# Sinkhorn attention into a routed expert layer: the last transposes of attention move to DMA, and loads, logits and sums move with them

## The chip, the core and the metric

One Trainium2 chip, one core. The engines named below are PE (TensorE: matrix products, with its weight loads PEld), DVE (VectorE), ACT (ScalarE), POOL (GpSimd) and SP (SyncE, which here only issues DMAs). The metric is the device time of one execution in microseconds (us); lower is better. Each engine runs its own instructions in the order in which they were built into its queue and waits, at an instruction, for semaphores that other engines or DMAs raise.

## The reference, cut to what matters

Two stages. The first is attention inside blocks of 96 rows, with the blocks of k and v mixed by an 8x8 matrix P per head; the second sends every row of the result x through all 8 experts, weighted by a balanced softmax.

```python
B, H, S, D = 4, 8, 768, 64               # P: 5 rounds of exp, row and column sums
k_sorted = einsum('bhij,bhjcd->bhicd', P, k_blocks)
v_sorted = einsum('bhij,bhjcd->bhicd', P, v_blocks)
attn = softmax(q_block @ k_sorted_block.T / 8)          # per block of 96
x = (attn @ v_sorted_block) as [B*S = 3072, H*D = 512]

logits = x @ w_gate                      # 8 experts
P = exp(logits - max)
for _ in range(8):                       # balance rows, then columns
    P /= P.sum(1); P /= P.sum(0); P *= N / E
for e in range(8):
    out += P[:, e:e+1] * (relu(x @ w1[e]) @ w2[e])      # 512 -> 1024 -> 512
```

## The kernel before

Batches are counted from 0 in the code, so "batches 3 and 4" of the change are the code's `bb` 2 and 3; below they are batch 2 and batch 3. A unit `hp` is a pair of heads (0 to 3).

**Attention of one batch.** `load_batch` (L70) fetches q, k and v of a batch from HBM as bf16; these DMAs are issued by POOL, each into one of five shared buffers `kvq`. `spread_r` (L151) makes R, the matrix P of the batch spread over 128 partitions, by two POOL multiplications (L139); R lies in two buffers used in turn by even and odd batches. `sort_values` (L162) multiplies v by R on PE (L165), ACT copies the result into `vs` (L167), and `hop` (L155) moves it by eight small DMAs into `vsb`, four issued by SP and four by POOL. Then, per head pair: `queries` (L174) has POOL lay out q again as `qr` (L186, two buffers), PE transpose it (L190) and ACT or DVE copy it out; `keys` (L196) multiplies k by R (L204), with the DVE copy L209; `scores` (L218) is L226 with the exp on ACT (L234); `mix` (L237) is L244, with DVE dividing by the row sums into `og` (L247, L248).

**Turning x.** The result `og` has rows on partitions; the expert stage wants it transposed, in `xtT`. `turn` (L252) does it with eight PE transposes into one PSUM bank and a DVE copy (L258); `turn_by_dma` (L260) has SP issue one transposing DMA (L261). `logits` (L268) multiplies `xtT` by the gate, 24 small matmuls (L275), and DVE copies them to `glog` (L279).

**The order of the work** is written by hand. A plan string per batch lists the steps of each group: `q`, `k`, `s`, `m` with a head pair, `t` for `turn`, `T` for `turn_by_dma`, `x` for one of the four DVE subtractions of `sum_x(0)` (L121, L128), `L` for all logits of the batch before, `l` for logits of this one. `weave` (L546) alternates the groups with steps of `ex`, which is the first expert's work on the batches already done (`hidden0` L402, `output0` L411). So PE goes back and forth between a batch's attention and expert 0 of the batch before. What is wrapped in `pin` keeps the order in which it was written on its engine; the rest (the copies to `qr`, the DMAs of `hop` for batches 2 and 3, the transposing DMAs) is placed by the scheduler. PSUM is eight banks in rotation (`pa`) during this stage, then split anew into five (`bk`) and three (`op`).

**The first expert's tail.** The loop at L873 has 56 steps: `last_two` does expert 0 for batches 2 and 3, `balance` (L653, the eight rounds of the router's P on `glog`, one PE matmul L681 and some DVE operations per round) is advanced at the steps listed at L883, and `hiddens` starts the other experts at step 27. `scale0` (L829) scales expert 0's outputs on ACT once P is final; `sums(8)` (L887) starts the POOL sums of the second weights, held back by a small copy of `glog`. After the loop the seven other experts follow, with seven products in place of eight for each 2x2 block product: some 500 us in which nothing is changed.

Of the kernel before, what the change touches and what calls it, by code (L numbers as in the profile page):

```python
# [25 lines left out]
def kernel(  # L26
# [14 lines left out]
    N, Dm, E, F = 3072, 512, 8, 1024  # L41
    NT = 24
    TB = S // 128
# [26 lines left out]
    def load_batch(bb, parts):  # L70
        for x, l0, n in parts:
            d, src = {"v": (vt, v), "k": (kt, k), "q": (qt, q)}[x]
            if bb not in d:
                d[bb] = kvp.tile([128, 8, 384], BF16, name="kvq", bufs=5)
            pin(nc.gpsimd.dma_start(
                out=d[bb][:, l0:l0 + n, :],
                in_=src[bb, l0:l0 + n].rearrange("h (p kk) d -> p h (kk d)", kk=6)))
# [43 lines left out]
    def sum_x(p):  # L121
        if p not in xc:
            xc[p] = xcp.tile([128, 3, 2, 512], BF16, name="xc", bufs=2)
        ta, tb = (slice(1024 * p + 512 * i, 1024 * p + 512 * i + 512) for i in range(2))
        b11, b12, b21, b22 = (xtT[:, k:k + 2, t] for k in (0, 2) for t in (ta, tb))
        x1, x2, x4 = (xc[p][:, j] for j in range(3))
        for a, b, c in ((b12, b11, x1), (b22, x1, x2), (b21, x2, x4), (b22, b12, b12)):
            pin(nc.vector.tensor_tensor(out=c, in0=a, in1=b, op=ALU.subtract))  # L128
            yield
# [4 lines left out]
    def build_r(bb, eng, n, pbps=None):  # L134

        Rt[bb] = perp.tile([128, 8, 8, 16], BF16, name=f"R{bb % 2}")
        for h in range(0, 8, n):
            yield
            ins = eng.tensor_tensor(  # L139
                out=mkap(Rt[bb], [Rt[bb].ap[0], [16, 8 * n], [1, 16]] if pbps is None else  # L140
                         [Rt[bb].ap[0], [128, n], [16, 8], [1, 16]], off=h * 128),
                in0=(mkap(Pb, [Pb.ap[0], [1, 8 * n], [0, 16]], off=(bb * 8 + h) * 8)
                     if pbps is None else
                     mkap(pbps, [pbps.ap[0], [1, n], [32, 8], [0, 16]], off=h)),
                in1=mkap(mask16, [mask16.ap[0], [0, 8 * n], [1, 16]] if pbps is None else
                         [mask16.ap[0], [0, n], [0, 8], [1, 16]]),
                op=ALU.mult)
            pin(ins)


    def spread_r(bb):  # L151
        for _ in build_r(bb, nc.gpsimd, 4):
            pass
# [59 lines left out]
    x0 = sum_x(0)  # L213
# [54 lines left out]
    def logits(bb, bank, ks):  # L268

        if 0 in ks:  # L270
            gp[bb] = bank([128, TB, E], F32)
        for kk in ks:
            for t in range(TB):
                c = bb * S + t * 128
                pin(nc.tensor.matmul(gp[bb][:, t, :], xtT[:, kk, c:c + 128], wg[:, kk],  # L275
                                     start=(kk == 0 and t == 0), stop=(kk == 3),
                                     skip_group_check=True))
        if 3 in ks:
            nc.vector.tensor_copy(glog[:, bb * TB:(bb + 1) * TB, :], gp[bb])  # L279
# [122 lines left out]
    def hidden0(c0, hTs, hbank, fbs=range(8)):  # L402
        for fb in fbs:
            hps = hbank()
            for kk in range(4):
                pin(nc.tensor.matmul(hps[:, 0:384], w1t[0][:, kk, fb * 128:(fb + 1) * 128],  # L406
                                     xtT[:, kk, c0:c0 + 384], start=(kk == 0), stop=(kk == 3)))
            nc.scalar.activation(out=hTs[:, fb, 0:384], in_=hps[:, 0:384], func=AF.Relu)
            yield

    def output0(c0, hTs, obank, done, tts=range(3)):  # L411
        for tt in tts:
            oacc = obank()
            for fb in range(8):
                pin(nc.tensor.matmul(oacc, hTs[:, fb, tt * 128:(tt + 1) * 128],  # L415
                                     w2t[0][:, fb, :], start=(fb == 0), stop=(fb == 7)))
                if fb == 3:
                    yield
            done(c0 // 128 + tt, oacc)
            yield  # L420
# [21 lines left out]
    with tc.tile_pool(name="ps0", bufs=4, space=bass.MemoryType.PSUM,  # L442
# [71 lines left out]
        for x in ("s00 k2 s01 k3 p s02 s03 m00 s10 m01 s11 m02 t00 m03 s12 m10 t01 s13 h00 m11 "  # L514
                  "g00 m12 h01 g01 m13 t10 h02 g02 t11 h03 g03 v0 v1 v2 v3 h10 g10 l").split():
            n = [int(c) for c in x[1:]]
# [10 lines left out]
            elif x[0] == "g":  # L527
                b, g, t = *n, part[x[1:]]
# [17 lines left out]
    def weave(a, b, na, nb):  # L546

        t = 0
        for i in range(na):
            next(a, 0)  # L550
            while t * na < (i + 1) * nb:
                next(b, 0)
                t += 1

    with ExitStack() as c2:
        pa = c2.enter_context(tc.tile_pool(name="pa", bufs=8, space=bass.MemoryType.PSUM,
                                           reuse_waits="tile"))
        bank1 = lambda shape, dt: pa.tile(shape, dt, name="bank", tag="bank")
        ebank = lambda: bank1([128, 512], F32)
        def by_turns(x, y):  # L560
            for a, b in ((x, y), (x, y)):
                yield next(a)
                yield next(b)

        def first_two():
            yield from hidden0(384, halves[1], ebank, range(2, 8))
            for c0, hTs in ((0, halves[0]), (384, halves[1])):
                o = [output0(c0, hTs, ebank, keep, (tt,)) for tt in range(3)]
                if c0 == 0:
                    yield from by_turns(o[0], o[1])  # L570
                    yield from o[2]
                else:
                    for one in o:
                        yield from one
            for c0 in (S, S + 384):
                hTs = mps.tile([128, 8, 384], BF16, name="hTs")
                yield from hidden0(c0, hTs, ebank)
                yield from output0(c0, hTs, ebank, keep)

        ex = first_two()  # L580

        def run(n):
            for _ in range(n):
                next(ex)

        def run_both(a, counts):
            for n in counts:
                next(a, 0)
                run(n)

        at1 = attention(1, bank1, "k0 k1 q0 q1 s0 k2 q2 k3 q3 s1 s2 s3 "
                                  "m0 m1,t0 m2,t1 m3,t2 t3,l0 l3")
        run_both(at1, (1, 1, 1, 0, 1, 0, 0, 1, 0, 1, 0, 2))
        load_batch(2, [(x, 0, 8) for x in "vkq"])
        spread_r(2)
        run_both(at1, (2, 1, 1, 1))
        run_both(sort_values(2, bank1), (1, 0, 1, 0, 1))
        run_both(at1, (1, 1))
        for bb, plan, ns in (
                (2, "q0,q1,k0 q2,x0,k1,s0 q3,x0,k2,s1 m0,T0 k3,s2 m1,T1,x0 s3 m2,T2 m3,T3",  # L600
                 (6, 4, 2, 2)),
                (3, "q0,q1,k0 q2,k1,s0 q3,k2,s1 m0,T0 k3,s2,L0 m1,T1 s3 m2,T2 m3 t3,l0 l3",
                 (6, 4, 0, 4))):
            at1 = attention(bb, bank1, plan)
            weave(at1, ex, 5, ns[0])
            if bb + 1 < B:
                load_batch(bb + 1, [(x, 0, 8) for x in "vkq"])
                spread_r(bb + 1)
            else:
                load_w1(1)  # L610
                sums = sum_w(1)
            weave(at1, ex, 3, ns[1])
            if bb + 1 < B:
                weave(sort_values(bb + 1, bank1), ex, 5, ns[2])
            else:
                for _ in sums:
                    pass
            weave(at1, ex, 3 if bb == 3 else 1, ns[3])
        for _ in ex:
            pass  # L620
    actx.close()
# [15 lines left out]
    def bank():  # L637
        return bk.tile([128, 512], F32, name="bk")
# [190 lines left out]
    def scale0(ts):  # L829
        for t in ts:  # L830
            pin(nc.scalar.activation(out=acc(t), in_=acc(t), func=AF.Copy,
                                     scale=glog[:, t, 0:1]))
# [36 lines left out]
    tail0, chain, ahead = last_two(), balance(), hiddens()  # L869
    x1, x2 = sum_x(1), sum_x(2)  # L870
    works = {12: x0, 18: x1, 22: x1, 25: x1, 26: x1, 41: x2, 43: x2, 46: x2, 48: x2}
    scaled = {41: 0, 42: 4, 43: 1, 45: 5, 47: 2, 49: 6}
    for n in range(56):  # L873
        next(tail0)
        if n >= 27:
            next(ahead)
            if n == 50:
                sum_h(0, hTs[0], 0, 3)
        if n in works:
            next(works[n], 0)  # L880
        if n in scaled:
            scale0([scaled[n]])
        if n in (0, 2, 4, 7, 8, 12, 14, 17, 19, 22, 24, 26, 28, 30, 32, 34, 36, 38):  # L883
            next(chain)
        if n == 40:
            pin(nc.gpsimd.tensor_copy(held, glog[0:96, NT - 1, 0:2]))
            sums(8)  # L887

# [2 lines left out]
    for n in range(1, 3 * (E - 1) + 1):  # L891
        e, p, hT = 1 + (n - 1) // 3, (n - 1) % 3, hTs[n - 1]
# [55 lines left out]
```

## Time and profile before

| what | value |
|---|---|
| time, median of 3 runs | 667.61 us (667.38 to 668.79) |
| the profiled execution | 667.94 us, span 666.2 us |
| PE busy | 652.2 us, 98% of the span |
| DVE, POOL, ACT busy | 83%, 71%, 45% |
| attention and expert 0 of batches 0 to 3 | about 0 to 163 us |
| the seven other experts | from about 163 us to the end |

The span runs from the first to the last instruction; the execution's own time has some 1.7 us around it. In a row of the timeline the columns are the start in us, the length in us, the engine, the line, the operation, what it writes and reads, its sizes and the number of instructions merged into the row; a bracket tells how long the engine sat idle before it and what ended that.

### The profile page before, as it was taken

How to read it: one execution, taken by the hardware profiler on the slowest of the kernel's cores; microseconds unless marked ns; L12 is line 12 of the kernel's file. 1: busy time of each engine (PE TensorE's matmuls, PEld its weight loads, DVE VectorE, ACT ScalarE, POOL GpSimd, SP SyncE). 2: the span in 40 equal slices, each digit the busy share in tenths (PEclk: the TensorE clock that was granted, in tenths of full speed). 3: DMA queues.
4: the chain of work that ended last, by engine and by line, in shares of the span. 5: the costliest groups of instructions: out<-in, count | busy, mean ns of one | idle time of the engine just before them, and what ended most of it. 6: DMA issues, size and time to landing. Idle time of an engine off the chain costs nothing.

```text
span 666.2 us, 13041 instructions
## 1 busy us (share of the span) xinstructions
PE 652.2 (98%) x5007; PEld 432.8 (65%) x5084; DVE 555.3 (83%) x1120; ACT 300.5 (45%) x535; POOL 470.9 (71%) x500
## 2 busy tenths in 40 slices
PE   7999999999999999999999999999999999999997
PEld 3766665554666666666666666666666666666666
DVE  6655866785888898898989898989898989898996
ACT  5775874476455443333334333433343334333430
POOL 4713254037897898898897999689886999646652
PEclk9999999999999999999999999999999999999999
DMA  9998995003041240033103040034003120001124
GB/s 188 175 220 142 175 151 80 0 1 64 1 63 19 47 64 1 1 64 46 19 1 63 1 64 1 1 64 64 1 1 65 18 47 1 1 1 63 67 95 159
DMA packets 38975, 38.34 MB, mean 58 GB/s; under 512 B 7712, under 2 KB 32000, under 8 KB 38912
## 3 DMA queue, kind: packets, MB, share of 16 engines
q0 software_dynamic: 26784, 27.03, 25.8%
q1 hardware_dynamic: 12016, 10.36, 6.3%
q8 instruction: 40, 0.66, 0.4%
q14 instruction: 23, 0.19, 0.1%
q10 hardware_dynamic: 112, 0.10, 0.1%
HBM read 52.45 MB, written 6.29 MB: 88 GB/s over the span
## 4 chain that ended last, share of the span: by engine, by line
PE 94%; DVE 3%; issue 1%; ACT 1%; POOL 0%; DMA 0%; ACTq 0%; DVEq 0%
PE oacc L787 38%; PE bk L700 37%; PE oacc L415 3%; PE bk L406 3%; PE bank L415 3%; PE bank L406 2%; PE bank L244 1%; PE pair L370 1%; PE bank L204 1%; PE bk L787 1%; PE bank L226 1%; PE bk L823 1%; PE bank L165 0%; PE pair L346 0%; PE bank L190 0%
## 5 line engine op out<-in xcount | busy, mean ns | idle before, releaser
L752 DVE SCALAR_TENSOR_TENSOR osbl<-oacc,glog,osbl 128x256 f32<-128x256 f32 (+1 forms) x490 | 255.6, 523 | 27.9 <-PE oacc L787 18.4
L770 POOL TENSOR_TENSOR hs<-hT 128x512 bf16<-128x512 bf16 (+2 forms) x105 | 98.4, 949 | 73.6 <-DVE hT L718 73.6
L700 PE MATMUL bk<-xtT,w1e 128*128 128x512 bf16 x477 | 143.1, 379 | 1.1
L718 DVE CUSTOM_DVE_ANT_0 hT<-bk,p 128x512 bf16<-128x512 f32 x168 | 116.0, 691 | 28.0 <-PE bk L700 22.7
L787 PEld LDWEIGHTS <-hT 128*128 128x128 bf16 x996 | 97.4, 98 | 62.7 <-issue 0.2
L787 PEld LDWEIGHTS <-hs 128*128 128x128 bf16 x996 | 97.4, 98 | 61.2 <-issue 1.6
L787 PE MATMUL oacc<-w2e,hT 128*128 128x256 bf16 x796 | 119.7, 273 | 0.2
L723 ACT COPY p<-bk 128x512 f32<-128x512 f32 x84 | 49.2, 585 | 148.3 <-PE bk L700 145.6
L770 POOL TENSOR_TENSOR hs<-hT,hs 128x512 bf16<-128x512 bf16 (+2 forms) x105 | 99.3, 953 | 4.7
L770 POOL TENSOR_TENSOR hs<-hs,hT 128x512 bf16<-128x512 bf16 (+2 forms) x105 | 99.1, 953 | 4.5 <-ACT hT L745 0.2
L700 PE MATMUL bk<-xc,wc 128*128 128x512 bf16 x317 | 95.7, 379 | 0.5
L745 ACT ACTIVATE hT<-bk 128x512 bf16<-128x512 f32 x84 | 50.1, 597 | 95.6 <-PE bk L700 95.6
L787 PE MATMUL oacc<-w2e,hs 128*128 128x256 bf16 x612 | 91.8, 273 | 0.2
L700 PEld LDWEIGHTS <-w1e 128*128 128x128 bf16 x672 | 65.7, 98 | 12.1
L718 DVE CUSTOM_DVE_ANT_0 hT<-bk,u 128x512 bf16<-128x512 f32 x84 | 58.0, 690 | 3.2 <-PE bk L700 3.2
L746 DVE SCALAR_TENSOR_TENSOR h<-bk,hT 128x512 bf16<-128x512 f32 x84 | 57.1, 680 | 3.6 <-ACT hT L745 3.6
L727 ACT COPY u<-bk 128x512 f32<-128x512 f32 x84 | 49.2, 585 | 24.0 <-PE bk L700 20.9
L732 ACT COPY p<-bk 128x512 f32<-128x512 f32 x84 | 49.2, 586 | 23.2 <-PE bk L700 23.2
L700 PEld LDWEIGHTS <-wc 128*128 128x128 bf16 x504 | 49.3, 98 | 8.1 <-issue 0.3
L787 PE MATMUL oacc<-w2s,hs 128*128 128x256 bf16 x364 | 53.3, 272 | 0.2
L700 PE MATMUL bk<-xc,w1e 128*128 128x512 bf16 x160 | 48.2, 379 | 0.4
L700 PE MATMUL bk<-xtT,wc 128*128 128x512 bf16 x158 | 47.8, 379 | 0.0
(146 smaller groups left out, 780.8 us busy)
## 6 DMA issues: line engine op xcount, KB each, us to landing
w1e<-in_moe_w_dram POOLq DMA_DIRECT2D x7, 1024.0 KB, 8.3
w2e<-in_moe_w_dram POOLq DMA_DIRECT2D x7, 1024.0 KB, 8.9
out_dram<-osbl SPq DMA_DIRECT2D x23, 256.0 KB, 2.2
kvq<-in_v_dram POOLq DMA_DIRECT2D x3, 768.0 KB, 10.1
kvq<-in_k_dram POOLq DMA_DIRECT2D x3, 768.0 KB, 11.3
vsb<-vs SPq DMA_DIRECT2D x18, 97.5 KB, 4.7
kvq<-in_q_dram POOLq DMA_DIRECT2D x4, 384.0 KB, 9.8
kvq<-in_q_dram POOLq DMA_DIRECT2D x2, 768.0 KB, 20.3
```

Of the source, the lines that this page charges most:

```text
L406: pin(nc.tensor.matmul(hps[:, 0:384], w1t[0][:, kk, fb * 128:(fb + 1) * 128], xtT[:, kk, c0:c0 + 384], start=(kk == 0), stop=(kk == 3)))
L415: pin(nc.tensor.matmul(oacc, hTs[:, fb, tt * 128:(tt + 1) * 128], w2t[0][:, fb, :], start=(fb == 0), stop=(fb == 7)))
L700: hold(nc.tensor.matmul(ps, wa[:, kk, :], xa[:, kk, :], start=(first and kk == 0), stop=(kk == 1), skip_group_check=True))
L718: nc.vector._custom_dve(TENSOR_ADD_SAT, out=out, in0=ps, in1=other, s0=TOP, s1=0.0)
L723: still(nc.scalar.copy(p1, u))
L727: still(nc.scalar.copy(u2, u))
L732: still(nc.scalar.copy(p5, v))
L745: still(nc.scalar.activation(out=c21, in_=u, func=AF.Relu))
L746: nc.vector.scalar_tensor_tensor(out=h3[e, p][:, i, :], in0=u, scalar=0.0, in1=c22, op0=ALU.max, op1=ALU.subtract)
L752: nc.vector.scalar_tensor_tensor(out=o, in0=ps, scalar=glog[:, t, e:e + 1], in1=o, op0=ALU.mult, op1=ALU.add)
L770: hold(nc.gpsimd.tensor_tensor(out=c, in0=a, in1=b, op=o))
L787: nc.tensor.matmul(ps, h[:, fb, :], w[:, fb, :], start=(first and fb == 0), stop=(fb == 3), skip_group_check=True)
```

## The change

Six edits, all in the order of work:

1. Head pair 3 of batch 3 is turned by a DMA as well (`T3`), where it was turned by PE and DVE (`t3`).
2. The logits of batch 3 leave the attention stage (`l0`, `l3`) and are computed after step 2 of the first expert's tail.
3. v of batch 3 is loaded by a call of its own, right after the loads of batch 2 and ahead of `spread_r(2)`; the later call loads k and q only.
4. In both plans the queries of head pairs 2 and 3 come later (`k1,s0` ahead of `q2`; `q3` with `m1`).
5. The three steps of `sum_x(0)` in batch 2's plan come later (with `s2`, `m1`, `s3`), and the logits of batch 2 move from `s2` to `s3` in batch 3's.
6. In the tail the rounds of `balance`, the scaling and the start of the POOL sums come 2 to 4 steps later; the numbers of `ex` steps woven in are changed by one here and there.

```diff
@@ -592,19 +592,20 @@
         load_batch(2, [(x, 0, 8) for x in "vkq"])
+        load_batch(3, [("v", 0, 8)])
         spread_r(2)
         run_both(at1, (2, 1, 1, 1))
         run_both(sort_values(2, bank1), (1, 0, 1, 0, 1))
         run_both(at1, (1, 1))
         for bb, plan, ns in (
-                (2, "q0,q1,k0 q2,x0,k1,s0 q3,x0,k2,s1 m0,T0 k3,s2 m1,T1,x0 s3 m2,T2 m3,T3",
-                 (6, 4, 2, 2)),
-                (3, "q0,q1,k0 q2,k1,s0 q3,k2,s1 m0,T0 k3,s2,L0 m1,T1 s3 m2,T2 m3 t3,l0 l3",
+                (2, "q0,q1,k0 k1,s0 q2,k2,s1 m0,T0 k3,s2,x0 q3,m1,T1,x0 s3,x0 m2,T2 m3,T3",
+                 (6, 3, 2, 3)),
+                (3, "q0,q1,k0 k1,s0 q2,k2,s1 m0,T0 k3,s2 q3,m1,T1 s3,L0 m2,T2 m3,T3",
                  (6, 4, 0, 4))):
             at1 = attention(bb, bank1, plan)
             weave(at1, ex, 5, ns[0])
             if bb + 1 < B:
-                load_batch(bb + 1, [(x, 0, 8) for x in "vkq"])
+                load_batch(bb + 1, [(x, 0, 8) for x in "kq"])
                 spread_r(bb + 1)
...
-            weave(at1, ex, 3 if bb == 3 else 1, ns[3])
+            weave(at1, ex, 1, ns[3])
@@ -869,9 +870,12 @@
-    scaled = {41: 0, 42: 4, 43: 1, 45: 5, 47: 2, 49: 6}
+    scaled = {43: 0, 44: 4, 45: 1, 47: 5, 49: 2, 51: 6}
     for n in range(56):
         next(tail0)
+        if n == 2:
+            logits(3, lambda shape, dt: bank()[:, 0:TB * E].rearrange(
+                "p (t e) -> p t e", e=E), range(4))
...
-        if n in (0, 2, 4, 7, 8, 12, 14, 17, 19, 22, 24, 26, 28, 30, 32, 34, 36, 38):
+        if n in (3, 5, 7, 10, 12, 16, 18, 21, 23, 25, 27, 29, 31, 33, 35, 37, 39, 41):
             next(chain)
-        if n == 40:
+        if n == 42:
             pin(nc.gpsimd.tensor_copy(held, glog[0:96, NT - 1, 0:2]))
             sums(8)
```

The order that the scheduler makes of it, on POOL, from the load of batch 2's q to the load of batch 3's q. Built before:

```
load q(2);  R(2) x2;  qr(2) x2;  hop(2) x4;  qr(2) x2;  load v(3), k(3), q(3)
```

and built after:

```
load q(2);  qr(2) x2;  load v(3);  R(2) x2;  hop(2) x4;  qr(2);  load k(3), q(3)
```

On PE the rows up to the first matmul of `sort_values(2)` stand in the same order in both.

## The prediction

> **What bounds the kernel now.** I read the page first, then PE's waits stage by stage, then the timelines of POOL and PE from 30 to 110 us.
>
> ```profile
> span 666.2 us, 13041 instructions
> PE 652.2 (98%) x5007; PEld 432.8 (65%) x5084; DVE 555.3 (83%) x1120; ACT 300.5 (45%) x535; POOL 470.9 (71%) x500
> PE 94%; DVE 3%; issue 1%; ACT 1%; POOL 0%; DMA 0%; ACTq 0%; DVEq 0%
> ```
>
> PE sets the end: 98% busy, 94% of the chain that ended last. So a microsecond in which PE newly stands still is a microsecond on the end, and what can be won is what PE idles or what is taken off PE. In the stretches from 56 to 107 us, where the edits lie, PE is busy 48.7 of 51.1 us by the table of stretches; the 2.4 idle lie in a few named waits:
>
> ```profile
> PE bk L406 <- DVE osbl L423: 0.8, 1, 0.8
> PE bank L190 <- POOL qr L186: 0.5, 1, 0.5
> PE bank L244 <- DVE kTs L209: 0.3, 1, 0.3
> PE bank L190 <- DVE osbl L423: 0.3, 1, 0.3
> ...
> PE bank L255 <- DVE og L248: 0.2, 1, 0.2
> ```
>
> (Columns: who waited for whom, us in total, times, longest.) That is the whole prize. The danger is in POOL's order, since POOL takes its queue in turn (the v load at 65.36 below needed nothing that was late and still stood behind the copies):
>
> ```profile
> 34.08 0.88 POOL L75 DMA_DIRECT2D kvq<-in_q_dram  x1 [3.95 <-PE pair L285]
> 34.97 2.08 POOL L139 TENSOR_TENSOR R<-Pb,mask 128x512 bf16<-128x512 f32 x2
> 58.92 1.59 POOL L186 COPY qr<-kvq 128x768 bf16<-128x768 bf16 x2 [21.87 <-DMA kvq<-in_q_dram]
> 61.56 2.16 POOL L158 DMA_DIRECT2D vsb<-vs  x4 [1.06 <-issue]
> 63.83 1.59 POOL L186 COPY qr<-kvq 128x768 bf16<-128x768 bf16 x2
> 65.36 0.92 POOL L75 DMA_DIRECT2D kvq<-in_v_dram  x1
> ...
> 68.05 2.56 POOL L139 TENSOR_TENSOR R<-Pb,mask 128x512 bf16<-128x512 f32 x2
> ```
>
> Batch 2's q is asked for at 34.08 and lands at 58.9. R of batch 2 is made at 34.97, ahead of the copy that waits 21.87 us for that q. PE uses this R for the sorting of v from 56.63 on:
>
> ```profile
> 55.76 1.03 PE L415 MATMUL bank<-w2e,hTs 128*128 128x512 bf16 x3
> 56.63 0.49 PE L165 MATMUL bank<-kvq,R 128*128 128x384 bf16 x2
> 56.95 1.03 PE L415 MATMUL bank<-w2e,hTs 128*128 128x512 bf16 x4
> ```
>
> **The load of v set apart (edit 3): the large term.** The built order puts both `qr` copies and the v load ahead of R(2) on POOL, because `spread_r` is pinned behind the new load and the copies are free to go before both. Every step has a row: q lands, 58.92; two copies, 1.59, to 60.51; issue of the v load, 0.92, to 61.4; the first half of R (heads 0 to 3, all that the first matmul needs), half of 2.56, to 62.7, or half of 2.08, to 62.5. PE's first weight load for L165 stood at 56.41, its matmul at 56.63; now both wait until about 62.6. **PE stands still 6.1 us** (5.9 to 6.3). The second half of R is there at 63.6 to 64.0; PE wants it after two more L165 pairs and four L415, 1.5 us on, at 64.1: no second stop. Behind the waiting matmul on PE lie the rest of the sorting, expert 0's matmuls and all of batch 2, which nothing else can do; ACT and DVE only wait for PE. None of it is made up later: from 110 us on PE is busy 9.9 of every 10 us.
>
> **The clock after the stop.** A stop this long stands nowhere in the trace; the longest after the start are under 1 us. The nearest row is the start, where PE comes out of idleness:
>
> ```profile
> 1.19 5.75 PE L337 MATMUL pair<-blank 128*128 128x512 bf16 x14 [1.19 <-DVE blank L104]
> ```
>
> These start 0.43 apart, while four 128x512 matmuls of L415 take 1.03, some 0.216 apart. So 13 steps of 0.41 instead of 0.216 lose 2.5 us in the first 5.75, although the granted clock reads 1.00 there. Bounds for the new stop: 0 (PE keeps its pace) and 2.5 (it starts as at the beginning). A 6 us stop is nearer to the start's idleness than to the sub-microsecond waits that show no slowing; I take 2.0, a little under the row, since short matmuls bound by weight loads slow less.
>
> The Trainium skill, "TensorE: Matmul & The Clock Gate", Part 1, speaks against the change here: half clock after one idle window of about 3.4 us, full clock again after a busy one, the windows running free. By its figures a 6.1 us stop would hold a whole window some 8 times in 10 and cost at least 1.7 us, an estimate from that page; the sum below would then end 0.3 us lower. The trace's slow start agrees in kind; the re-throttling itself is in no run here yet.
>
> **The last turn by DMA (edit 1).** Off PE: eight transposes, 0.51 (103.29 to the next matmul at 103.80), and the 0.15 wait for `og` before them; off DVE: one copy of 0.54. Gain 0.65. Added: one DMA on SP, whose issue takes 1.2, with nothing queued behind it that anyone needs before 160 us.
>
> **The last logits (edit 2).** The 24 matmuls and their copy are the same. PE now needs the transposed `og` after three `hidden0` steps. Counting from the end of m3's matmuls: sixteen L415 (3.45), three `hidden0` of 0.65, then 18 logits matmuls (0.45) that need only the earlier pairs: head pair 3 is read at 6.0. DVE finishes `og` about 2.0 after m3 (1.83 for its eight operations, behind one 0.69 copy), and the last transposing DMA landed 2.8 after its issue:
>
> ```profile
> L261 SPq DMA_TRANSPOSE xtT<-og x7: 1213/1243/2059, 72.5 to 101.2; - x7
> ...
> DMA to landing us min/median/max: 2.8/5.8/10.4
> ```
>
> So it lands at 4.8, covered by 1.2 us. The 10.4 was taken while k and q were being loaded; at 101.24, with that traffic gone, it was 2.8. I take 0; if the cover were gone, up to 6.4.
>
> **The change of PSUM pools.** PE's 0.8 wait at 107.08 was for the copy of the last output tile. Two bank allocations fewer shift the rotation: the first `hidden0` of the tail then waits for an `og` long done, only the second for that copy. It ends 4.2 after m3, the second starts at 4.1: 0.1 left, gain 0.7.
>
> **Queries later (edit 4).** The two waits of L190 (0.26 and 0.53 at 84.85 and 87.75) came from `qr` copies behind a q load that landed at 83.2 and behind four `hop` issues. Now the third and fourth copy are needed about 4 us later. Batch 3's k and q are issued some 5 us later than before but two in place of three; three took 15.9 from issue to the last landing, about 5.3 each, so q lands near 84, and PE wants it near 90: covered by 6 us, the stop itself being most of that. Gain 0.8 (0.3 to 0.8).
>
> **`sum_x` later (edit 5).** Its 0.67 to 1.1 us operations sat between the DVE copies of k; the 0.3 wait at 70.25 is theirs in part, but ACT, busy 5.4 of 6 us there, is close behind. Gain 0.15 (0 to 0.3).
>
> **The tail later (edit 6).** Same operations. One round of `balance` gets 16 matmuls of L415 (3.46) between its two PE products with a subtraction in between: 0.3 latency, 0.73, 0.6 and 1.83 on DVE, 3.5 in all. Loss 0.1. The POOL sums start about 2.2 us later; POOL idled 4.36 before 162.53, which hides it (cover gone: that much beyond 4.36 late into the second expert's products). The scaling moves inside ACT's idle time (45% busy over the span).
>
> **The sum.** +6.1 (stop) +2.0 (clock) +0.1 (tail) −0.65 (turn) −0.7 (pools) −0.8 (`qr`) −0.15 (`sum_x`) = **+5.9 us**. Against the profiled execution, 667.94 with a span of 666.2: 673.8, span 672.1. The median of the runs is 0.33 lower: **673.5**.
>
> **Rivals.**
> - *The stop without the clock.* PE keeps its pace through 6 us. For it: the granted clock reads 1.00 everywhere, and the waits of up to 0.9 us show no slow matmuls behind them. Against: the slow start. +3.9: 671.5. By the Trainium skill's page this is the case in which no idle window falls whole into the stop.
> - *The transposing DMA comes late.* Should it meet the weight loads, or take the 9.4 to 10.4 of 72 to 76 us, PE waits up to 6.4 more at the logits, and longer than its 1.2 us cover from a landing of 4.0 on. For it: three of seven took 6 us or more. Against: the last, in the quiet, took 2.8. I price it at 4 more: 677.5.
> - *Faster: R is in time.* One mechanism: q of batch 2 lands early enough that POOL's chain of 1.59, 0.92 and 1.28 ends before 56.41. It decides from a landing at 52.6 on; then only the gains count: −2.2, 665.4. Against it: 58.9 in the trace, nothing ahead of this load in the queue is changed, and even k, asked for before q, landed at 55.0 (29.19 and 25.8). A landing between, at about 55, would give no change.
>
> **Chances.** Forecast 0.62, no clock loss 0.22, late DMA 0.09, in time 0.05, between 0.02. All but the last two are slower by more than 0.2% (1.3 us, about what a measurement of this kernel can tell from no change): slower 0.93, same 0.02, faster 0.05. Range: low end from stop 5.9, clock 0, gains at their largest 2.45 (`sum_x` 0.3): +3.5, 671.1, taken to 670.6 for the run's own spread; high end from 6.3, 2.5, 0.1 and gains at their smallest 1.65: +7.2, 674.9, taken to 677.0 for half of the late DMA.
>
> **What would show it.** Right: POOL's `qr` copies at 58.9 and R at 61.4; an idle gap of about 6 us on PE before L165 put down to POOL R; L415 and L165 matmuls behind it at twice their spacing for some 4 us; no wait of 0.8 at the first tail matmul, none of L190 for `qr`; `logits` without a wait for DMA. Wrong: R on POOL near 35 us, or q landing near 52; L165 at full pace right behind the gap (no clock loss); a wait of L275 for the last transposing DMA.

## The result and the profile after

The changed kernel takes 674.31 us (median of 6 runs, 672.33 to 679.88), the kernel before, run beside it, 667.79 us (667.38 to 668.79): ratio 1.011, 95% interval 1.0067 to 1.0152, so it is slower, by some 1.1%. The profiled execution took 673.76 us, span 671.8, against the 673.8 and 672.1 that were worked out. That this one execution meets the sum so closely is in part luck: the six runs lie some 7.5 us apart, and their median is 0.8 above the 673.5 of the forecast.

The page of the changed kernel: the span, busy time by engine, the granted clock in 40 slices, and the shares of the chain that ended last.

```profile
span 671.8 us, 13104 instructions
PE 656.9 (98%) x5076; PEld 433.1 (64%) x5076; DVE 554.5 (83%) x1119; ACT 300.7 (45%) x535; POOL 470.5 (70%) x500
PEclk9997999999999999999999999999999999999999
PE 89%; ACT 0%; POOL 0%; DVE 0%; issue 0%; ACTq 0%
```

PE still sets the end at 98%. The busy time of PE grew by 4.7 us, although it has eight transposes less to do: weight loads, one for each matmul, went from 5084 to 5076. (PE's own count rose from 5007 to 5076 because 77 matmuls of before are not on record, so the busy times are not quite comparable.) One slice of the clock, the fourth (50 to 67 us), reads 7 where all others read 9. Slow matmuls count as busy, so a share of the loss hides in the busy column.

PE's waits between 36 and 120 us in the changed kernel (us in total, times, longest):

```profile
PE bank L165 <- POOL R L139: 6.2, 1, 6.2
PE bank L226 <- ACT hTs L408: 0.2, 1, 0.2
```

All waits that the prediction quoted from before are gone, and in their place stands one of 6.2. What made it is read from POOL's timeline of the changed kernel:

```profile
34.13 0.88 POOL L75 DMA_DIRECT2D kvq<-in_q_dram  x1 [3.95 <-PE pair L285]
59.52 1.59 POOL L186 COPY qr<-kvq 128x768 bf16<-128x768 bf16 x2 [24.51 <-DMA kvq<-in_q_dram]
61.05 0.87 POOL L75 DMA_DIRECT2D kvq<-in_v_dram  x1
61.94 2.07 POOL L139 TENSOR_TENSOR R<-Pb,mask 128x512 bf16<-128x512 f32 x2
```

R of batch 2, which was made at 34.97 before, is made at 61.94: behind the v load, which stands behind two copies that wait for q until 59.52. The timeline of PE shows the wait and what follows it:

```profile
55.81 1.03 PE L415 MATMUL bank<-w2e,hTs 128*128 128x512 bf16 x4
63.07 0.82 PE L165 MATMUL bank<-kvq,R 128*128 128x384 bf16 x2 [6.23 <-POOL R L139]
63.68 1.91 PE L415 MATMUL bank<-w2e,hTs 128*128 128x512 bf16 x4
65.39 1.49 PE L165 MATMUL bank<-kvq,R 128*128 128x384 bf16 x4
66.67 1.18 PE L415 MATMUL bank<-w2e,hTs 128*128 128x512 bf16 x4
67.69 0.49 PE L165 MATMUL bank<-kvq,R 128*128 128x384 bf16 x2
```

Four matmuls of L415 take 1.03 us ahead of the stop, 1.91 behind it, and are back near 1.03 at 67. The table of stretches gives the clock for it (length, busy us and instructions of PE, PEld, DVE, ACT and POOL, then the granted clock, the DMA share and GB/s):

```profile
56.84:60.20 3.36, 0.00 (x0) 0.00 (x0) 1.11 (x3) 0.00 (x0) 0.68 (x1) 0.99 0.36 55
60.20:63.07 2.87, 0.00 (x1) 0.01 (x1) 0.00 (x0) 0.00 (x0) 2.85 (x5) 0.50 0.19 6
63.07:67.00 3.93, 3.93 (x11) 1.63 (x12) 0.00 (x0) 2.24 (x6) 0.94 (x1) 0.50 1.18 172
67.00:69.00 2.00, 2.00 (x13) 1.00 (x12) 0.00 (x0) 1.64 (x4) 0.00 (x0) 1.00 0.30 46
```

PE idles, 3.4 us later the clock falls to half, and it comes back 6.8 us after that; 3.93 us of work are done at half pace, which loses up to 1.97.

At the other end of the change, the first expert's tail on PE's timeline of the changed kernel, and the transposing DMAs:

```profile
111.74 2.41 PE L406 MATMUL bk<-xtT,w1e 128*128 128x384 bf16 x12
113.99 0.75 PE L275 MATMUL bk<-wg,xtT 128*128 128x8 bf16 x24
```
```profile
L261 SPq DMA_TRANSPOSE xtT<-og x8: 1213/1240/2360, 80.1 to 110.6; - x8
DMA to landing us min/median/max: 2.8/4.4/8.5
```

The moved logits run without a wait for the transposing DMA.

Where the time went, row by row, after minus before: the first L165 of batch 2 comes 6.44 later (63.07 against 56.63), the first L190 of batch 2 8.36 later (71.55 against 63.19), so 1.92 are the clock's. The tail starts 4.66 later (111.74 against 107.08), with the 0.60 of logits still to come: 5.26 for equal work, so attention won 3.1 back. The span ends 5.6 later; the tail lost 0.34, nearly all of it in its first row: those twelve L406 take 2.41, where the first twelve of before's tail take 2.11 once they run.

### The profile page after: what moved, and what is told of

Its sections match the earlier page's. It is cut to its first block, busy times and chain, and to the rows that moved or that the text cites. A ratio compares the mean times of both kernels' runs of the same rounds, so it can differ in the third digit from the quotient of the medians.

```text
span 671.8 us, 13104 instructions
## 1 busy us (share of the span) xinstructions
PE 656.9 (98%) x5076; PEld 433.1 (64%) x5076; DVE 554.5 (83%) x1119; ACT 300.7 (45%) x535; POOL 470.5 (70%) x500
## 4 chain that ended last, share of the span: by engine, by line
PE 89%; ACT 0%; POOL 0%; DVE 0%; issue 0%; ACTq 0%
PE bk L701 38%; PE oacc L788 37%; PE oacc L415 3%; PE bk L406 3%; PE bank L415 2%; PE bank L406 2%; PE bank L244 1%; PE bk L788 1%; PE bank L226 1%; PE bank L165 1%; PE bank L204 1%; PE bk L824 1%; PE bank L190 0%; PE bank L275 0%; ACT atp L234 0%; POOL R L139 0%
## 5 line engine op out<-in xcount | busy, mean ns | idle before, releaser
L701 PE MATMUL bk<-xtT,w1e 128*128 128x512 bf16 x504 | 148.6, 379 | 0.0
L701 PE MATMUL bk<-xc,wc 128*128 128x512 bf16 x336 | 99.8, 379 | 0.1
L701 PE MATMUL bk<-xc,w1e 128*128 128x512 bf16 x168 | 50.0, 379 | 0.0
L701 PE MATMUL bk<-xtT,wc 128*128 128x512 bf16 x168 | 50.0, 379 | 0.0
## 6 DMA issues: line engine op xcount, KB each, us to landing
vsb<-vs SPq DMA_DIRECT2D x18, 97.5 KB, 5.1
```

Of the source, the lines that this page charges most:

```text
L701: hold(nc.tensor.matmul(ps, wa[:, kk, :], xa[:, kk, :], start=(first and kk == 0), stop=(kk == 1), skip_group_check=True))
```

## The experiments

"After" stands for the changed kernel, and its edits have the numbers of the list above. Each run is compared with the kernel before on the same chip; the median of before was 668.2 to 668.4 in all of them.

**The changed kernel once more (`again`).**

> The changed kernel once more, for a second profile and more runs. Theory: 672 to 680 us; if the profiled run is long, the half-clock stretch behind the stop is longer than the 4.2 us of the first profile, about 2 us of it for each us lost, with q landing at 58.9 to 59.5 as before. Rival: q lands later by as much as the run is longer, with the same half-clock stretch.

673.44 us, ratio 1.0074 (1.006 to 1.0088), clock 0.994, the same 6.2 us wait and half clock from 60 to 67. The four runs lie within 0.2 us. None of them was as long as the 678.2 and 679.9 us of two of the first six, of which only the clock is known (0.992 and 0.990); where in those runs it was lost stays open.

**Edit 3 alone (`v_alone`): the kernel before with v of batch 3 loaded apart.**

```diff
         load_batch(2, [(x, 0, 8) for x in "vkq"])
+        load_batch(3, [("v", 0, 8)])
         spread_r(2)
...
-                load_batch(bb + 1, [(x, 0, 8) for x in "vkq"])
+                load_batch(bb + 1, [(x, 0, 8) for x in "kq"])
```

> The kernel before with edit 3 alone: batch 3's v loaded apart ahead of R(2), all else as before. Theory: the copies of q go ahead of R(2) on POOL, PE stops some 6.3 us at L165 and runs at half clock for some 4 us; none of the gains of the other edits except that the two waits for qr shrink: 675.5 us (673.5 to 682, as wide as the changed kernel's own runs). Rival (the loss comes from the other edits): 667.8 us, no stop.

676.98 us, ratio 1.0131 (1.0105 to 1.0156). PE waits 5.9 us for R, and the profiled span is 6.9 us longer than before's 666.2. Edit 3 alone makes more than the whole loss; the five others win some of it back (3.5 us between the medians of this and the run above, 1.4 between the two profiled spans; the four runs of this one lie 4.3 us apart). With the old plans PE also waits 0.9 for a transposing DMA here, in spite of the stop.

**The stop without its clock (`fill`): 36 products of zeros on PE while it waits for R**, into a bank that is overwritten afterwards. They need nothing that is late.

```diff
             vps = bank([128, 384], F32)
+            if bb == 2 and h == 0:
+                for _ in range(36):
+                    pin(nc.tensor.matmul(vps, blank[:, 0:128], blank[:, 0:384],
+                                         start=True, stop=True))
```

> The changed kernel with 36 matmuls of zeros (384 columns) on PE ahead of the sorting of v of batch 2, into the bank that the first real matmul then overwrites: some 5.9 us of work inside the stop. Theory (the clock falls because PE stands idle): the stop stays, L165 starts at about 63 us, but L165 and L415 behind it run at full pace (four L415 in 1.03 in place of 1.91): 672.2 us (671.5 to 672.8), and the runs lie within 1.5 us of each other if the spread of the changed kernel (672.3 to 679.9) is the clock's. Rival (the spread is in the landing of q, or the slow matmuls behind the stop have another cause than the idleness): 674 us or more in the middle, runs as far apart as 7 us.

671.67 us (671.15 to 671.85, all five at clock 1.000), ratio 1.0045 (1.0032 to 1.0058): 1.8 us less than the changed kernel beside it. The wait for R shrinks to what the zeros leave of it, and the stretch behind it runs at full clock (the added lines make L165 L169 here):

```profile
PE bank L169 <- POOL R L139: 0.4, 1, 0.4
63.00:65.00 2.00, 1.99 (x11) 1.09 (x12) 0.00 (x0) 1.46 (x4) 0.97 (x1) 1.00 1.03 126
```

The first real matmul starts at 63.01, as late as in `again` (62.92), and four matmuls of expert 0 behind it take 1.03 again. More work on PE makes the kernel faster, because PE does not fall to half clock.

**The stop taken away (`r_first`): R of batch 2 ahead of the new load.** Two lines change places.

```diff
-        load_batch(3, [("v", 0, 8)])
         spread_r(2)
+        load_batch(3, [("v", 0, 8)])
```

> The changed kernel with one pair of calls swapped: R of batch 2 is spread ahead of the load of batch 3's v, which puts R(2) on POOL ahead of the copies that wait for q, as before the change. Theory (the loss is the stop of PE for R plus the half clock behind it, and everything else in the change gains 2.3 to 2.6 us): 665.2 us (664.6 to 665.8), no wait of L165 for POOL, clock 1.00 throughout, runs within 1.5 us of each other. Rival (another edit costs as well, the last transposing DMA or the logits behind it): above 667 us, with the wait on L275.

669.47 us (666.27 to 673.18, 12 runs), ratio 1.0006 (0.9981 to 1.003), where 665.2 was expected. The wait for R is gone and 4.0 us with it (673.44 for `again` beside it), but not the 8 that stop and clock had cost. PE's waits from 36 to 120 us in this kernel tell why:

```profile
PE bank L244 <- DMA vsb<-vs: 2.4, 1, 2.4
PE bank L226 <- ACT hTs L408: 0.2, 1, 0.2
```

The first `mix` of batch 2 waits for a `hop`. On POOL of this kernel the v load is now issued just ahead of the hops:

```profile
60.91 0.94 POOL L75 DMA_DIRECT2D kvq<-in_v_dram  x1
61.84 2.10 POOL L158 DMA_DIRECT2D vsb<-vs  x4
```

and the eight hops of batch 2 land (last number: median us from issue to landing) in 7.1 and 9.7 us, first fence, where before they took 3.8 and 3.7, second fence:

```profile
vsb<-vs SPq DMA_DIRECT2D x4, 97.5 KB, 7.1
vsb<-vs POOLq DMA_DIRECT2D x4, 97.5 KB, 9.7
```
```profile
vsb<-vs SPq DMA_DIRECT2D x4, 97.5 KB, 3.8
vsb<-vs POOLq DMA_DIRECT2D x4, 97.5 KB, 3.7
```

So edit 3 costs in a second place, which the 6 us stop had hidden: there the v load had landed (7.1 us after its issue at 61.05) before the hops were issued. This agrees with the Trainium skill, "DMA: Bandwidth & Descriptors", Queues, rings and completion order, by which each DMA engine goes round between the queues that have work: a small transfer that SP issues shares the engines with the large one. Those that POOL issues on the load's own queue were the slower ones. The 2.4 us wait brings the half clock too, 3.4 us of it (74.0 to 77.3).

**The values behind the hops (`v_after_hop`)**: edit 3's load moved behind `sort_values(2)` and the two steps after it.

> The changed kernel with the values of batch 3 still loaded apart and early, but issued by POOL behind the four hops of batch 2 that it issues, not ahead of R and the hops. Theory (what costs in the second place is a load that is issued ahead of the hops): hops land in 3.7 to 4.5 us, no wait on R, at most 0.5 us on the hops, and 665 to 666 us. Rival (the two share the DMA engines, in whatever order they are issued): hops of 5 us and more, a wait of 1 us or more ahead of the first mix, 667 us or more. If POOL's later issue of the load holds up the third copy of queries behind it, a wait of under 1 us shows at the queries' transposes and the time is between the two.

666.82 us (665.18 to 674.41), ratio 0.9994 (0.9969 to 1.0018). Batch 2's hops land in 4.8 (SP) and 3.6 us (POOL), PE waits neither for R nor for them: order of issue decides most of it (`vah_qk` below has the same order here and one wait of 0.7 for a hop). What is left are waits of 0.8 and 0.3 us at the queries of batch 3.

**Without edit 3 (`v_joined`): v, k and q of batch 3 together, as before.**

> The changed kernel without its edit 3: the values of batch 3 come with its keys and queries as before, R of batch 2 is first on POOL again and nothing is loaded beside batch 2's hops. Theory (edit 3 costs in two places, the R that waits on POOL and, once that is mended, the hops of batch 2 that share the DMA engines with the values of batch 3): no wait of PE on R or on the hops, hops landing in about 3.8 us as before, no slice of lower clock around 60 to 78 us, and the gain of the other edits without any loss: before's own time less 2.2 to 2.9, which is 664.9 to 665.6 us, ratio 0.995 to 0.997. Rival (the later queries alone bring the first mix of batch 2 too near to the hops, whoever loads beside them): PE still waits 1 to 2.5 us on the hops ahead of that mix and the time is 667 to 669, as with R first.

669.99 us (666.70 to 671.03), ratio 1.0013 (0.9999 to 1.0027): not the 665 expected. R and the hops (3.9 and 3.5 us) are in time as the theory has it, and the rival is wrong as well; a third thing is late. PE's waits in this kernel:

```profile
PE bank L190 <- POOL qr L186: 2.6, 2, 2.4
PE bank L226 <- ACT hTs L408: 0.2, 1, 0.2
```

The transposes of batch 3's queries wait for the copies on POOL, and these for q, third of three loads, which landed 18.8 us after its issue at 66.31. Here edit 3 may have its use: with v early, q landed at 80.8 (`r_first`) and 83.7 (`v_after_hop`), here at 85.1. One profile of each doesn't settle it, for with the three together it landed at 82.7 in `j_old_plans` below. Behind the stop stands the half clock again, 3.4 us long, in the stretches of this kernel:

```profile
84.60:88.00 3.40, 1.58 (x25) 1.15 (x26) 0.23 (x1) 1.24 (x2) 2.72 (x5) 1.00 1.22 132
88.00:91.40 3.40, 3.40 (x26) 1.76 (x26) 1.28 (x3) 1.31 (x3) 3.35 (x5) 0.50 0.91 187
91.40:93.00 1.60, 1.60 (x32) 1.18 (x30) 0.60 (x2) 1.27 (x4) 0.00 (x0) 1.00 0.75 94
```

**Without edit 3 and with the old end (`j_old_end`)**: on `v_joined`, the last turn by PE and batch 3's logits in the attention stage (the last count of woven steps goes back with them).

```diff
-                (3, "... q3,m1,T1 s3,L0 m2,T2 m3,T3",
+                (3, "... q3,m1,T1 s3,L0 m2,T2 m3 t3,l0 l3",
...
-        if n == 2:
-            logits(3, ...)
```

> Like the kernel whose values come together (v_joined), with the end of batch 3 as before: the last turn by matmuls, its logits at the end of the attention and not in the tail. Expected from the prediction's terms (turn 0.65 and the idle time at the change of PSUM pools 0.7): 1.35 us over v_joined, about 666.6, with a turn of eight matmuls in the page again and idle time of PE of some 0.8 us ahead of the first hidden layer of the tail. Rival (the transposing transfer's late landing eats what it saves): within 0.4 us of v_joined.

669.64 us, ratio 1.0018 (1.0 to 1.0036), span 667.9 against 667.8: edits 1 and 2 win nothing that can be seen. Their tail starts 1.0 earlier (107.83 against 108.83), and from there to the end takes 0.9 longer (559.97 against 559.07): 0.6 for the logits' own time, 0.3 more in the first twelve L406 of `v_joined` (2.41 again). The stop at the queries is 2.1 us in one and 2.6 in the other, so the equal spans price the end only roughly. Two by-products. The 0.8 wait at the first tail matmul is not there with the old end either, so the banks saved by edits 1 and 2 are not needed to remove it. And the tail with edit 6 but without the logits is as long as before's (559.07 against 559.12), so edit 6 costs nothing.

**Without edit 3 and with the old plans (`j_old_plans`)**: on `v_joined`, edits 4 and 5 undone.

```diff
-                (2, "q0,q1,k0 k1,s0 q2,k2,s1 m0,T0 k3,s2,x0 q3,m1,T1,x0 s3,x0 m2,T2 m3,T3",
-                 (6, 3, 2, 3)),
-                (3, "q0,q1,k0 k1,s0 q2,k2,s1 m0,T0 k3,s2 q3,m1,T1 s3,L0 m2,T2 m3,T3",
+                (2, "q0,q1,k0 q2,x0,k1,s0 q3,x0,k2,s1 m0,T0 k3,s2 m1,T1,x0 s3 m2,T2 m3,T3",
+                 (6, 4, 2, 2)),
+                (3, "q0,q1,k0 q2,k1,s0 q3,k2,s1 m0,T0 k3,s2,L0 m1,T1 s3 m2,T2 m3,T3",
```

> Like v_joined, with the two plans of batch 2 and 3 as before (queries two stages earlier, sums over x at their old places), the last turn still by the transposing transfer. Expected from the prediction's terms (0.8 of waits for the copies of queries, 0.15 of the sums): 0.95 us over v_joined, about 666.2, with waits of PE for POOL's copies of queries of 0.5 and 0.3 us in the trace again. Rival (the engine that waits there makes it up later): within 0.3 us of v_joined.

667.17 us, ratio 0.9988 (0.9975 to 1.0): 2.8 faster than `v_joined`, not 0.95 slower. The waits of 0.5 and 0.2 for the copies are back, as expected, and there is one of 1.0 for a transposing DMA, but q landed in 15.6 us and the stop of 2.4 isn't there. So without edit 3 the later queries gain nothing by themselves; what decides is whether q has landed when PE comes to it. It isn't one profile's luck: 9 of the 12 runs of `v_joined` have a clock of 0.997, and 3 of the 12 here. Why q landed sooner isn't known.

**q ahead of k, two ways.** k goes straight to PE, q through a POOL copy of 0.83 per head pair, so q is needed sooner. `vah_qk` is `v_after_hop` with the late pair loaded as q, k; `j_vqk` is `v_joined` with v, q, k, whose edit is shown:

```diff
-                load_batch(bb + 1, [(x, 0, 8) for x in "vkq"])
+                load_batch(bb + 1, [(x, 0, 8) for x in "vqk"])
```

> The kernel with the values of batch 3 behind the hops (v_after_hop), with the queries of batch 3 asked for ahead of the keys. Theory (with the stop gone, PE reaches batch 3's first transposes of queries at 83.8 us, while q, last of the three loads, lands at 83.65 and still needs POOL's copy of 0.83): q as the second of three lands near 80, k near 83.7 and is first used after the queries, so the waits of 0.8 and 0.3 us at the queries' transposes go and nothing comes in their place: profiled span 663.6 to 664.0 where the clock is 1.00, time 665.3 to 665.9, ratio to before 0.996 to 0.998. Rival (k becomes the wait instead, of 0.5 to 1 us, at the first product of keys of batch 3): no gain, 666.4 to 667.

> The kernel whose values of batch 3 come with its keys and queries (v_joined), asked for in the order v, q, k in place of v, k, q. Theory (v_joined's 2.4 us stop and the half clock behind it come from q's landing, 18.8 us after its issue, as the last of three): q lands some 4 us earlier, near 81, the stop at the queries' transposes is under 0.3 us; k lands near 85 where PE wants it near 84.9, a wait of 0 to 0.5; no half clock, 665.5 to 666.5 us. Rival (the whole stop moves to the keys): 2 us of waiting at the first product of keys and 669 to 670 us as in v_joined.

`j_vqk`: 666.66 us (665.22 to 674.85), ratio 0.9983 (0.9954 to 1.0013), span of the profile 664.4 at clock 1.000. The stop at the queries is gone (q landed in 11.2, k in 15.7), 0.8 is left at the logits of batch 2. `vah_qk`: 670.18 us (665.99 to 675.06), ratio 1.0022 (0.999 to 1.0053), against the theory, though the waits of q are gone as it says. Its timeline of PE shows what was late instead, batch 2's logits waiting for the last transposing DMA:

```profile
96.78 0.61 PE L275 MATMUL bank<-wg,xtT 128*128 128x8 bf16 x18
100.99 0.33 PE L275 MATMUL bank<-wg,xtT 128*128 128x8 bf16 x6 [3.61 <-DMA xtT<-og]
```

A transposing DMA took up to 15.1 us here, issued while w1 of the second expert (1 MB) was loading; another wait for such a DMA, 1.6 us, stands at the tail's logits. The 1.6 is the late transposing DMA of the prediction's second rival, priced at 4 there; the 3.6 is another one of its kind, batch 2's last, of which the prediction says nothing.

**Batch 2's logits one stage later (`j_vqk_l0`), and w1 later as well (`j_vqk_l0_w1`).**

```diff
-                (3, "... q3,m1,T1 s3,L0 m2,T2 m3,T3",
+                (3, "... q3,m1,T1 s3 m2,T2,L0 m3,T3",
```

> The kernel with v, q, k of batch 3 together in that order (j_vqk), and batch 2's logits one stage later in batch 3's plan (with m2 in place of s3). Theory (with the stop gone what is late is the transposing transfer of batch 2's last head pair, issued near 85.7 while w1 of expert 1 is loading, landing 11.9 to 15.1 us later; its landing differs from run to run and PE's wait for it brings the lower clock): the logits now come some 3.5 us later, near 101, so PE waits for no transposing transfer; profiled span near 663.5 at clock 1.00, fewer runs above 668, median 665.5 to 666.3, ratio 0.996 to 0.998. Rival (the spread of the runs has another cause, such as the chip's own throttle or the loads of q): the 0.8 us wait goes, but a third of the runs is still at 668 and more and the ratio is not apart from 1.

> As j_vqk_l0, and the load of the second expert's w1 is asked for behind the three further stages of batch 3, some 8 us later. Theory (it is this load that holds up batch 2's last transposing transfers): those issued from 85 on land in 3 to 6 us; but the last one of batch 3, issued near 103, may now meet the load: then PE waits 1 to 3 us at the tail's logits and the time is 666.5 to 668; if it lands in time, 665.3 to 666. Rival (the transfers hold up each other, not the load): landings of 10 us and more as before.

666.36 us (665.34 to 676.02), ratio 0.9953 (0.9924 to 0.9982), and 665.85 us (665.10 to 670.56), ratio 0.9964 (0.994 to 0.9989); before beside them 668.37. The second edit hardly did what it says: POOL runs ahead of PE and issued the load at 86.00 in place of 85.19, so the two are nearly one kernel, and whether that load holds up the transfers stays open. By the medians they are 2.0 and 2.5 us (0.3 and 0.4%) faster than before, near the 2.2 of gains that the prediction counted, and both are clearly faster than the changed kernel. Against before only the second is shown to be faster: the interval of the first is without its two longest runs, 675.84 and 676.02, and with them its mean of 668.3 is not told apart from before's 669.3. But their profiled executions each hold a stop, and not the same one. Waits of the first, then of the second:

```profile
PE bank L204 <- DMA kvq<-in_k_dram: 2.0, 1, 2.0
```
```profile
PE bank L275 <- DMA xtT<-og: 2.6, 1, 2.6
```

In the first, no slice shows a lower clock and the span is 665.5; in the second PE does 5.4 us at half clock behind the stop, and the span is 668.8. The wait of the second is the one that moving the logits was meant to clear: they came only 1.6 us later than in `j_vqk` (97.85 against 96.27), not 3.5, and the transfer took 16.1. The DMA answers show why the runs of one kernel differ. The load of k of batch 3, third of three, in `j_vqk`, `j_vqk_l0` and `j_vqk_l0_w1`, whose orders on POOL and PE are the same up to this point:

```profile
kvq<-in_k_dram POOLq DMA_DIRECT2D x1, 768.0 KB, 15.7
```
```profile
kvq<-in_k_dram POOLq DMA_DIRECT2D x1, 768.0 KB, 20.1
```
```profile
kvq<-in_k_dram POOLq DMA_DIRECT2D x1, 768.0 KB, 16.1
```

Landings 4 us apart decide in these profiles whether PE stops; where it does, the clock can nearly double the price. The single runs fit that: in `j_vqk_l0` the eight runs at clock 0.999 to 1.000 took 665.3 to 667.6 us, the four at 0.992 to 0.997 took 669.2 to 676.0. They do not show it, for they have no trace, and the kernel before has such runs too: of the 23 beside these, four at 0.992 to 0.997 took 670.9 to 675.3. What makes a landing vary isn't known.

## Why the prediction was right, step by step

- **R behind the v load: right.** 6.1 predicted, 6.2 waited. Copies 0.6 later than assumed (q landed at 59.5, not 58.9), the first half of R shorter; the second half made no stop, as said. `v_alone` shows that edit 3 suffices, `r_first` that POOL's order is the cause.
- **The clock: right, in size too.** 2.0 predicted, 1.92 by the rows, 1.8 by `fill`. The 1.00 that the prediction read at the start, as a point for its first rival, was no measurement: the clock's record begins with a rise, at 6.40 in before and at 5.54 in the changed kernel, and there the slow matmuls of L337 become fast (in the changed kernel from 0.43 apart to 0.22). The start was at half clock. The sum by the Trainium skill's page (at least 1.7, 8 in 10) was as good. Its rule ("TensorE: Matmul & The Clock Gate", Part 1) agrees with the 3.36 idle at full clock and the 6.8 at half in "after"; but it speaks of a window of idleness, and the table of `v_joined` above differs: half clock behind 3.40 us in which PE was busy for 1.58. Every profiled stop of 2.1 or more brought it, one of 2.0 did not. Where a stop lies may count as well as its length: in all eight profiles with half clock behind a stop, it begins a whole number of steps of 3.41 us behind that first rise (16 in the changed kernel: 60.15 behind 5.54; 20 in `r_first`, 24 in `v_joined`, 28 in `vah_qk`) and ends one or two steps later. The stop of 2.0, in `j_vqk_l0`, was cut in two by such a step, with 0.98 us of idle time ahead of it and 1.01 behind.
- **The gains: right, 0.6 too small.** 2.3 predicted in attention, 3.1 measured, 0.34 of it given back in the tail, where 0.1 was predicted: 2.8 net against 2.2. Of the 3.1, 2.16 is idle time of PE that is gone (2.26 us of it from 63.19 to 107.08 in before, 0.10 from 71.55 to 111.74 in "after"), which holds all five waits that the prediction named, and 0.51 is the turn's matmuls. The other 0.4 is shorter busy time, whose cause stays open.
- **The change of PSUM pools: right as a mechanism, mis-sized.** In the programs as built, expert 0's last output of before lies in bank 0, which the first `hidden0` of the tail gets too; in "after" it lies in bank 4, which the second one gets, as the prediction said. It put what is left of the wait at 0.1; the rows say 0.3 (2.41 against 2.11), and that is the loss in the tail. Fewer allocations are one way to move that bank, not the only one: in `j_old_end`, with none fewer, the new plans put that output in bank 2, which the fifth `hidden0` gets.
- **Queries later: right with a condition that the prediction named and priced too low.** It said of the cover of q "the stop itself being most of that". In "after" q landed at 87.8, not near 84, and PE came to it at 92.1. One of the two waits it counted (0.26) the profile puts on a bank that DVE was still emptying (L423), not on the copies; both are gone. With the stop gone, `v_joined` lost 2.4 there, and half clock with it.
- **The transposing DMA covered: right for "after"** (no wait of L275). Without the stop PE waited for such a DMA in four profiled kernels (`j_vqk` 0.8, `j_old_plans` 1.0, `j_vqk_l0_w1` 2.6, `vah_qk` 3.6 and 1.6), only the last of these at the tail's logits, and did not in `r_first`, `v_joined`, `v_after_hop` and `j_vqk_l0`. That the stop had given the DMAs peace is not shown: `v_alone` has the stop and waited 0.9.
- **The rival "R in time", 665.4: right as a size, not as a switch.** With R in time and nothing else changed the median was 669.5, and only the runs at clock 1.000 came to 666.3 to 666.7. The prediction overlooked that the v load would then meet the hops.

## What to carry over

An engine that takes its queue in turn makes the place of a DMA issue a dependency: a load put ahead of a small product which the main engine waits for can cost more than all that its earlier data bring. Here the load itself waited for nothing that the profile shows; two copies that waited for q came to stand ahead of it, and the product behind all three. When a stop is taken away, look for what it gave time to: here the hops, q, k and the transposing DMAs were each late in one kernel or another, and most of the gain came out only after their order and their users' places had been set anew. Judge such versions by the clock of the single runs as well as by the median: a stop of some 2 us can cost nearly twice its length.

## What the runs showed of the hardware

Half clock came in stretches of 3.4 us (`r_first`, `v_joined`, `j_old_end`, stops of 2.1 to 2.4) or 6.8 (the changed kernel with its stop of 6.2, but `j_vqk_l0_w1` too with 2.6). How much idle time in the 3.4 us ahead brings it is open: 1.2 us was enough in `j_vqk_l0_w1` (96.25 to 99.66), while 1.7 right behind the first rise was not in `j_old_end` (4.29 to 7.70). A DMA of 97.5 KB between tiles took 3.5 to 4.0 us in the quiet and 7.1 to 9.7 right behind a load of 768 KB; put ahead of that load it took 3.6 to 4.8. The transposing DMA landed in 2.8 us at best and in 16.1 at worst, and a load of one size landed 15.7 to 20.1 us after its issue in kernels that were the same up to there.
